# Zero matmuls ahead of and between the first transposes, alpha loaded one step ahead, small loads later

## The chip, the cores and the metric

One core of a Trainium2 chip runs the kernel. TensorE (PE, with its weight loads shown as PEld), VectorE (DVE), ScalarE (ACT), GpSimd (POOL) and SyncE (SP) run side by side and wait for each other by semaphores; SP issues nearly all loads and stores to the DMA queue. The metric is device microseconds of one execution, lower is better.

## The reference

A linear attention with a decaying state feeds a mixture of experts with one expert per token. Batch 4, 8 heads, 768 tokens, 48 channels per head; 3072 tokens of 384 channels and 8 experts of 384 x 1024 x 384 behind it. All inputs are float32.

```python
for t in range(S):
    state = alpha[:, :, t, :, None] * state + np.einsum('bhd,bhe->bhde', k[:, :, t], v[:, :, t])
    y[:, :, t] = np.einsum('bhd,bhde->bhe', q[:, :, t], state)
...
logits = x @ w_gate + modality_bias[modality_id]
e_idx = np.argmax(logits, axis=1)
...
for e in range(E):
    mask = e_idx == e
    h = np.maximum(x[mask] @ w1[e], 0.0)
    out[mask] = gate_w[mask, None] * (h @ w2[e])
```

## The kernel before

The attention is done in 24 chunks of 128 tokens (six to each batch), in a software pipeline of 24 steps. Each chunk needs four loads of 192 KB: alpha, k, q and v, as 128 tokens by 8 heads by 48 channels. Step s of the loop (line 836) does this:

- issue the loads of a later chunk (line 838), ahead of all else of the step;
- `decay_in(s)`: TensorE transposes the four tiles of alpha chunk s (`trans`, L238) and the result is copied to `X` by ScalarE (L245; for chunk 0 by VectorE). In step 1 it comes behind `scale(0)`;
- `scale(s-1)`: TensorE transposes k and q of chunk s-1, VectorE multiplies them with the running products of alpha (L277 gives `kh`, L280 gives `qh`);
- `rows(s-3)`, and `logits_rows` in every second step: transposes of earlier results;
- `natural(s-1)`: TensorE transposes `kh` back (L286);
- `decay(s)`, `decay_back(s)`, `guard(s)`: two scans on VectorE (L250, L261) and a check of alpha on ScalarE (L265);
- `logits(s-3)` in every second step, from step 4 on (L368, reads `wgp`), `state(s-2)` (L318; nothing for the first chunk of a batch), `scores(s-1)` (L298), `outputs(s-2)` (L325, needs v of chunk s-2), `update(s-1)` (L343, needs v of chunk s-1).

TensorE, VectorE and ScalarE run in the order in which this is written out (`manual_schedule`). SP and GpSimd run in an order that a planner makes from the written order and its own idea of when things are ready. Each engine's instructions run strictly in its order, so one that waits holds back everything behind it.

Ahead of the loop, SP issues the load of `wgs` (the gate weights in a layout that only a fallback path reads, `logits_pe`), then twelve chunk loads in the order a0 k0 q0 a1 v0 k1 q1 a2 v1 k2 q2 v2, then six small ones: `wgp` in four pieces (the gate weights that `logits` reads), `mi` (modality of each token) and `mbb` (the bias table); the last two are read by `bias_table` in step 6. In step s > 0 it loads all four tensors of chunk s+2 (PF is 3). There are four buffers each for alpha, k and q and six for v, so chunk 3 has a buffer of its own from the start.

The router's work on earlier chunks is spread over the later steps. After the loop the experts run: weights are fetched as soon as the router knows which, and the matmuls of L987 to L1008 fill TensorE for the rest of the time.

`y` names a PSUM buffer of two banks that exists once; `state` takes it in step 2 for the first time.

## Time and profile before

| | |
|---|---|
| runs | 379.71, 376.4 and 588.9 us, median 379.71 |
| profiled execution | 379.2 us, of it 377.2 us span |
| mean granted TensorE clock | 0.988 |
| TensorE busy | 359.6 us, 95% of the span |
| VectorE, ScalarE, GpSimd busy | 59%, 50%, 40% |
| DMA | 59.19 MB, mean 157 GB/s |

Times in rows of the trace count from the start of the span. A row of the time line gives start, length, engine, line, operation, output tile from input tiles, and how many instructions were merged into it; in brackets stands the idle time of the engine ahead of it and what ended that. `SPq` rows are issues of the DMA queue: their length is that of the issue, not of the transfer. A matmul's row contains the time until its result is out, so neighbouring matmuls overlap; the distance of their starts is what one costs. PEclk is the clock granted to TensorE as a share of full speed.

### The profile page before, as it was taken

The page shows a single profiled execution, that of the slowest core. Times are in us where ns is not written, and L with a number is a line of the kernel's source. Part 1 is how long each engine was busy: PE and PEld are TensorE (multiplying, and loading weights), DVE is VectorE, ACT ScalarE, POOL GpSimd, SP SyncE. Part 2 cuts the span into 40 slices and gives each one's busy share as a digit, 9 for nine tenths or more (in the row PEclk, how much of TensorE's full clock was granted, in tenths as well). Part 3 has the DMA queues.
Part 4 walks back from the last instruction along what each step waited for, and adds up shares of the span by engine and source line. Part 5 has one row for each costly group of instructions (what it writes and reads, how often), then busy time and mean ns, then how long its engine had stood idle before and what let it go on. Part 6 is the DMA issues. An engine that isn't in the chain of part 4 may idle for free. (4 is left out here: it accounts for less than half of the span.)

```text
span 377.2 us, 9342 instructions
## 1 busy us (share of the span) xinstructions
PE 359.6 (95%) x3652; PEld 319.9 (85%) x3652; DVE 223.9 (59%) x454; ACT 189.4 (50%) x367; POOL 149.7 (40%) x218
## 2 busy tenths in 40 slices
PE   4979999999999989999999999999999999999993
PEld 3778789888888978789998899899889989888993
DVE  5765988977988988895846604641552366026400
ACT  2447677767767746344745415432552445145310
POOL 9434335434454544346155424612631273220022
PEclk9989999999999989999999999999999999999998
DMA  9999999999989792948847434621733373200011
GB/s 128 131 170 163 191 193 196 182 182 198 191 179 185 153 370 73 365 137 318 305 113 235 126 119 150 223 89 63 257 99 105 115 219 117 85 28 27 1 44 49
DMA packets 123246, 59.19 MB, mean 157 GB/s; under 512 B 103377, under 2 KB 114696, under 8 KB 123192
## 3 DMA queue, kind: packets, MB, share of 16 engines
q1 hardware_dynamic: 119224, 48.84, 57.1%
q0 software_dynamic: 3968, 9.65, 7.6%
q8 instruction: 31, 0.51, 0.6%
q14 instruction: 23, 0.19, 0.2%
HBM read 49.03 MB, written 9.50 MB: 155 GB/s over the span
## 5 line engine op out<-in xcount | busy, mean ns | idle before, releaser
L303 POOL TENSOR_SCALAR_AFFINE_SELECT scT<-scT 128x512 f32<-128x512 f32 x48 | 38.3, 821 | 72.4 <-ACT scT L302 72.4
L953 POOL DMA_INDIRECT out_dram<-os,odx x23 | 23.1, 1003 | 109.8 <-ACT os L1021 93.6
L987 PE MATMUL sc<-w2H,hH 128*128 128x384 f32 x192 | 65.0, 338 | 0.0
L989 PE MATMUL sc<-w2H,hL 128*128 128x384 f32 x192 | 64.2, 334 | 0.0
L988 PE MATMUL sc<-w2L,hH 128*128 128x384 f32 x192 | 64.1, 334 | 0.0
L823 DVE TENSOR_TENSOR w1L<-w1r,w1H 128x768 fp32r<-128x768 f32 x24 | 22.0, 956 | 67.2 <-ACT w1H L821 67.2
L1006 PE MATMUL tr<-xH,w1H 128*128 128x512 f32 (+1 forms) x144 | 53.8, 374 | 0.0
L1008 PE MATMUL tr<-xH,w1L 128*128 128x512 f32 (+1 forms) x144 | 53.5, 372 | 0.0
L1007 PE MATMUL tr<-xL,w1H 128*128 128x512 f32 (+1 forms) x144 | 53.5, 371 | 0.0
L815 DVE SCALAR_TENSOR_TENSOR hL<-tr,hH 128x512 fp32r<-128x512 f32 x47 | 32.4, 688 | 31.4 <-ACT hH L813 31.3
L813 ACT ACTIVATE hH<-tr 128x512 fp32r<-128x512 f32 x47 | 28.1, 598 | 45.4 <-PE tr L1008 42.0
L1021 ACT ACTIVATE os<-sc,gg 128x384 f32<-128x384 f32 x23 | 13.4, 583 | 67.0 <-PE sc L989 40.3
L987 PEld LDWEIGHTS sc<-w2H,hH 128*128 128x128 f32 x192 | 36.1, 188 | 1.1 <-issue 1.0
L988 PEld LDWEIGHTS sc<-w2L,hH 128*128 128x128 f32 x192 | 36.1, 188 | 0.0
L989 PEld LDWEIGHTS sc<-w2H,hL 128*128 128x128 f32 x192 | 36.0, 188 | 0.0
L686 POOL DMA_INDIRECT gg<-gd,idx x25 | 27.0, 1081 | 21.2 <-DMA gd<-gs 14.2
L302 ACT COPY scT<-sc 128x512 f32<-128x512 f32 x48 | 25.8, 590 | 13.6 <-PE sc L298 13.6
L261 DVE TENSOR_TENSOR_SCAN Fw<-X,DF 128x516 f32<-128x516 f32 x24 | 31.1, 1295 | 0.8
L680 POOL DMA_INDIRECT xg<-xd,idx x25 | 26.8, 1072 | 11.6 <-issue 5.2
L1008 PEld LDWEIGHTS tr<-xH,w1L 128*128 128x128 f32 x144 | 27.1, 188 | 4.7
L1007 PEld LDWEIGHTS tr<-xL,w1H 128*128 128x128 f32 x144 | 27.1, 188 | 4.6
L1006 PEld LDWEIGHTS tr<-xH,w1H 128*128 128x128 f32 x144 | 27.1, 188 | 4.7
(242 smaller groups left out, 682.9 us busy)
## 6 DMA issues: line engine op xcount, KB each, us to landing
w1r<-in_moe_w_dram SPq DMA_DIRECT2D x16, 768.0 KB, 4.6
w2r<-in_moe_w_dram SPq DMA_DIRECT2D x16, 768.0 KB, 7.8
nat_a<-in_alpha_dram SPq DMA_DIRECT2D x24, 192.0 KB, 4.1
nat_k<-in_k_dram SPq DMA_DIRECT2D x24, 192.0 KB, 5.5
nat_q<-in_q_dram SPq DMA_DIRECT2D x24, 192.0 KB, 4.2
vt<-in_v_dram SPq DMA_DIRECT2D x24, 192.0 KB, 5.1
xd<-xs SPq DMA_DIRECT2D x24, 192.0 KB, 3.9
xg<-xd,idx POOLq DMA_INDIRECT x25, 4.6
```

The source lines that it names most:

```text
L261: vec.tensor_tensor_scan(Fw, x[:, :-1], d, 0.0, op0=ALU.mult, op1=ALU.add)
L303: pool.affine_select(s, s, [[0, NP], [1, P]], ALU.is_ge, 0.0, base=0, channel_multiplier=-1)
L680: pool.indirect_dma_start(xg[x][:, u], None, xd[0:rows], IOA(idx[:, c : c + 1], 0), bounds_check=rows - 1, oob_is_err=False)
L686: pool.indirect_dma_start(gg[x][:, u : u + 1], None, gd[0:rows], IOA(idx[:, c : c + 1], 0), bounds_check=rows - 1, oob_is_err=False)
L813: act.activation(hH, hp, AF.Relu)
L815: vec.scalar_tensor_tensor(hL, hp, 0.0, hH.bitcast(F32), op0=ALU.max, op1=ALU.subtract)
L987: pe.matmul(op, hH[:, us] if f is None else hH[:, f, us], wH, start=first, stop=False)
L988: pe.matmul(op, hH[:, us] if f is None else hH[:, f, us], wL, start=False, stop=False)
L989: pe.matmul(op, hL[:, us] if f is None else hL[:, f, us], wH, start=False, stop=final)
L1006: pe.matmul(hp, wH[:, d, fs], XH[:, d, :n], start=(d == 0), stop=False)
L1007: pe.matmul(hp, wH[:, d, fs], XL[:, d, :n], start=False, stop=False)
L1008: pe.matmul(hp, wL[:, d, fs], XH[:, d, :n], start=False, stop=(d == ND - 1))
```

## The change

The load of `wgs` moves into the fallback path, which does not run with these inputs. Thirteen chunk loads are issued ahead of the loop, alpha one chunk further than the rest: a0 k0 q0 a1 v0 a2 k1 q1 v1 a3 k2 q2 v2. In the loop alpha of chunk s+3 and k, q, v of chunk s+2 are loaded. The `wgp` loads move into step 1, behind that step's chunk loads, and those of `mi` and `mbb` into step 2.

In addition VectorE clears a bf16 tile `still` of 128 x 512 ahead of its other work, and TensorE multiplies it with its own first 128 columns: seven times ahead of everything else, and once behind each of the first seven transposed chunks (a0, k0, q0, a1, a2, k1, q1). The products go to a tile `idle` in the `y` buffer, which nothing reads.

```diff
     wgs = cp.tile([P, ND, E], F32, name="wgs")
-    sp.dma_start(wgs, wg.rearrange("(c p) e -> p c e", p=P))
-
+    for n in "a0 k0 q0 a1 v0 a2 k1 q1 v1 a3 k2 q2 v2".split():
+        load(int(n[1]), n[0])
+    still = ac.tile([P, 4 * P], BF16, name="still")
+    vec.memset(still, 0.0)
+    idle = ps.tile([P, 4 * P], F32, name="y")
+
+    def warm(n):
+        for _ in range(n):
+            pe.matmul(idle, still[:, :P], still, start=True, stop=True)
+
+    warm(7)
     wgp = ac.tile([P, 2, 2, 32], F32, name="wgp")
     pool.memset(wgp, 0.0)
-    for n in "a0 k0 q0 a1 v0 k1 q1 a2 v1 k2 q2 v2".split():
-        load(int(n[1]), n[0])
-    for c in range(2):
-        ...
     mi = ac.tile([NU, P, 2], I32, name="mi")
-    sp.dma_start(mi.rearrange("t p w -> t (p w)"), ...)
     mbb = ac.tile([P, NM, E], F32, name="mbb")
-    sp.dma_start(mbb, mb.unsqueeze(0).broadcast_to([P, NM, E]))
+    def load_gate():
+        ...
+    def load_modality():
+        ...
@@ trans
+        if i < 2 or (i == 2 and n == "a"):
+            warm(1)
         return p
@@ general (fallback path)
+        sp.dma_start(wgs, wg.rearrange("(c p) e -> p c e", p=P))
@@ the loop over steps
     for s in range(NU):
+        if s > 0 and s + PF < NU:
+            load(s + PF, "a")
         if s > 0 and s + PF - 1 < NU:
-            load(s + PF - 1)
+            load(s + PF - 1, "kqv")
+        if s == 1:
+            load_gate()
+        if s == 2:
+            load_modality()
```

`load_gate` and `load_modality` hold the loads taken out above, four and two.

## The prediction

> **What bounds the kernel now.** First the page's list of engines. TensorE is busy for nearly the whole span, so time is gained by taking idle time, or slow time, away from TensorE. (The page's chain that ended last is only 1 us long here and says nothing.)

> ```profile
> PE 359.6 (95%) x3652; PEld 319.9 (85%) x3652; DVE 223.9 (59%) x454; ACT 189.4 (50%) x367; POOL 149.7 (40%) x218
> ```

> Second, TensorE's own time line. A row is a run of matmuls: start, length, line, how many, and in brackets the idle time before it. I measure from one start to the next, since the ends overlap.

> ```profile
> 4.96 1.08 PE L238 MATMUL tr<-ident,nat_a 128*128 128x128 f32 x4 [4.96 <-POOL zr L184]
> ...
> 10.38 1.12 PE L286 MATMUL tr<-ident,kh 128*128 128x128 f32 x4 [0.70 <-DVE kh L277]
> 11.42 1.99 PE L298 MATMUL sc<-qh,kh 48*64 48x128 f32 x32
> 13.34 1.09 PE L343 MATMUL kv<-vt,knat 128*64 128x48 f32 x16
> 14.36 1.12 PE L238 MATMUL tr<-ident,nat_a 128*128 128x128 f32 x4
> ...
> 17.21 0.63 PE L286 MATMUL tr<-ident,kh 128*128 128x128 f32 x4 [0.24 <-DVE kh L277]
> ...
> 19.72 0.62 PE L343 MATMUL kv<-vt,knat 128*64 128x48 f32 x16
> 22.41 0.63 PE L238 MATMUL tr<-ident,nat_a 128*128 128x128 f32 x4 [2.06 <-DMA nat_a<-in_alpha_dram]
> ...
> 29.27 0.65 PE L238 MATMUL tr<-ident,nat_a 128*128 128x128 f32 x4
> ...
> 30.63 0.62 PE L356 MATMUL tr<-ident,yt 128*128 128x128 f32 x4
> 31.14 0.66 PE L286 MATMUL tr<-ident,kh 128*128 128x128 f32 x4
> 31.73 0.64 PE L368 MATMUL kv<-yt,wgp 128*32 128x256 f32 x8
> 32.30 0.67 PE L318 MATMUL y<-qh,T 64*64 64x128 f32 x16
> 32.78 1.06 PE L298 MATMUL sc<-qh,kh 48*64 48x128 f32 x32
> 33.77 1.09 PE L325 MATMUL y<-scT,vt 128*64 128x128 f32 x16
> 34.70 0.62 PE L343 MATMUL kv<-vt,knat 128*64 128x48 f32 x16
> 35.25 0.66 PE L238 MATMUL tr<-ident,nat_a 128*128 128x128 f32 x4
> ```

> Step 4 runs from 29.27 to 35.25 with no gap: 5.98 us of TensorE work set its length. The beginning is different: transposing four tiles takes 1.12 us at 10.38 and 0.63 us at 17.21, and there is an idle stretch of 2.06 us ahead of alpha chunk 3, the first work of step 3 (22.41). So the first 17 us run on a slow clock, and at 22.41 a load is late.

> Third, the windows. Columns: window, its length, busy time of PE, PEld, DVE, ACT, POOL (instructions), granted clock, DMA share, GB/s. The cuts are 3.41 us apart, where the recorded clock changes.

> ```profile
> 6.37:9.78 3.41, 3.03 (x12) 1.86 (x10) 3.27 (x6) 0.60 (x3) 3.25 (x11) 1.00 1.50 166
> 9.78:13.19 3.41, 2.81 (x36) 2.31 (x36) 3.31 (x6) 1.71 (x4) 2.65 (x9) 1.00 1.50 163
> 13.19:16.60 3.41, 3.41 (x32) 3.17 (x28) 0.85 (x2) 1.93 (x4) 1.71 (x3) 1.00 1.46 160
> 20.02:23.43 3.41, 1.35 (x22) 1.25 (x19) 0.50 (x1) 1.09 (x4) 2.59 (x4) 1.00 0.95 151
> 23.43:26.85 3.42, 3.42 (x33) 3.09 (x35) 3.17 (x6) 1.58 (x4) 0.00 (x0) 0.50 1.19 178
> 40.50:43.91 3.41, 2.56 (x33) 2.19 (x33) 3.31 (x9) 2.43 (x7) 2.22 (x4) 1.00 1.22 204
> 132.66:136.07 3.41, 1.78 (x36) 1.11 (x37) 3.24 (x12) 1.05 (x3) 0.36 (x1) 1.00 1.03 380
> 136.07:139.49 3.42, 3.42 (x56) 3.09 (x58) 3.32 (x14) 1.53 (x6) 1.89 (x2) 0.50 1.06 384
> ```

> Read each row with the next one. After windows with TensorE busy for 1.35 of 3.41 us (40%) and 1.78 (52%) the clock is 0.50 for one window; after 2.56 (75%) it stays at 1.00. From 0.50 it comes back after a window that is full (3.42). The 1.00 of the first three rows can't be right: by the durations above TensorE was at about half speed until some 16.6. Windows filled to 89% (3.03) and 82% (2.81) did not open the clock; the full one, 13.19 to 16.60, did.

> Fourth, the load queue, for the late load.

> ```profile
> 0.81 0.44 SPq L136 DMA_DIRECT2D wgs<-in_moe_w_gate_dram  x1
> 1.30 0.48 SPq L133 DMA_DIRECT2D nat_a<-in_alpha_dram  x1
> ...
> 10.39 1.14 SPq L133 DMA_DIRECT2D nat_k<-in_k_dram  x1
> ...
> 12.76 1.14 SPq L133 DMA_DIRECT2D vt<-in_v_dram  x1
> 14.02 2.49 SPq L144 DMA_DIRECT2D wgp<-in_moe_w_gate_dram  x4
> 16.55 0.43 SPq L149 DMA_DIRECT2D mi<-in_moe_modality_id_dram  x1
> 17.42 0.43 SPq L133 DMA_DIRECT2D nat_a<-in_alpha_dram  x1
> ```

> Alpha chunk 3 is issued at 17.42, behind twelve chunk loads (1.19 us apart) and six small loads that hold the queue from 14.02 to 17.42; TensorE gets it at 22.41, 4.99 us after its issue.

> **The change, part by part.** *Loads.* The wgs load leaves the front: the first chunk is issued up to 1.30 - 0.81 = 0.49 us earlier (at least 0, if it then waits for something else). Alpha 3 becomes the tenth load; the tenth was issued at 10.39, so it goes at about 9.9 and lands near 14.9.

> *Warm matmuls at the front.* VectorE first clears `still`; its first memset now is this:

> ```profile
> 0.99 0.49 DVE L155 MEMSET DR<- 128x517 f32 x1 [0.99 <-PEq L1220]
> ```

> With as long a one the seven matmuls start near 1.5, and all transposes stand behind them. No bf16 matmul of 512 columns is in this trace. Nearest are fp32r ones of 384 columns:

> ```profile
> 175.68 0.33 PE L989 MATMUL sc<-w2H,hL 128*128 128x384 f32 x1
> ...
> 177.76 0.34 PE L989 MATMUL sc<-w2H,hL 128*128 128x384 f32 x1
> ```

> Twelve starts in 2.08 us are 0.173 us each, hence 0.23 us for 512 columns at full clock and 0.46 at half (a bound below is 0.17, as if columns cost nothing; above, 0.46 at any clock). Seven at half clock are 3.2 us: 1.5 to 4.7. The first alpha lands up to 0.49 before 4.96, so its transposes start near 4.7: I take 0.25 us of gain at the front (bounds 0 and 0.49). From 1.5 on TensorE is without a gap of note until the clock opens, after the first full window of 3.41 us: between 4.9 and 8.3, since the start of the windows need not lie the same in another execution.

> *Steps 0 to 2.* In step 0 and the first half of step 1 VectorE is what is late (the brackets at 10.38 and 17.21 name its `kh`). Its scan ahead of the second kh:

> ```profile
> 12.58 1.23 DVE L261 TENSOR_TENSOR_SCAN Fw<-X,DF 128x516 f32<-128x516 f32 x1
> ```

> So a faster TensorE gains nothing before `kh`, and the four warm matmuls among the first transposes lie beside this wait. The transposes of kh start at 10.38 - 0.25 = 10.13. From there at full clock, with step 4's lengths: natural 0.59 (31.14 to 31.73; was 1.04), scores 0.99 (was 1.92), update 0.55 (was 1.02), so step 2 begins at 12.26 instead of 14.36. Its three transposed chunks take 1.36 (29.27 to 30.63) plus three warm matmuls of 0.23, to 14.3. That is just behind the second kh, which VectorE can make by then (its scan ends at 12.58 + 1.23 - 0.25 = 13.56). From natural to the end of update took 17.21 to 20.27 (19.72 + 0.55), 3.06 us, and with 0.1 for qh step 3 begins at 17.5. Here chunk 3 (landed at 14.9) is no longer late. So the gain to this point is 22.41 - 17.5 = 4.9 us, of which 2.1 are the late load and 2.8 the clock and the front.

> *Step 3.* It took 29.27 - 22.41 = 6.86 us, half of it at half clock. With no idle stretch ahead the clock need not fall: its length is then step 4's without the logits, 5.98 - 0.57 = 5.41. Gain 1.45.

> *The moved small loads.* The wgp loads come after 17 chunk loads instead of 12: issued from 14.02 + 5 x 1.19 - 0.49 = 19.5 to 22.0. The last row gives what they took from issue to landing (from the view of the tile wgp); the first, of the queue's time line, is a chunk load that held the queue 1.0 us longer than the usual 1.1:

> ```profile
> 19.59 2.15 SPq L133 DMA_DIRECT2D vt<-in_v_dram  x1
> ```

> ```profile
> DMA to landing us min/median/max: 3.0/3.5/3.9
> ```

> So the last, issued near 21.6 (22.0 less the 0.43 of one issue), lands at 24.6 to 25.5. Logits of step 4 want it at 17.5 + 5.41 + 2.46 (29.27 to 31.73) = 25.4. All of step 4 from state on stands behind them in TensorE's order. The bounds of the wait are 0 and 1.1 (the late landing with one such long issue ahead of it); I take the middle, 0.5. The other step 4 and 5 loads have 2 us or more in hand by the same count, and mi and mbb, wanted in step 6, more.

> `idle` lies in the `y` buffer of PSUM, which only TensorE writes before step 2, in its own order: no cost. After step 4 TensorE is the engine that sets the pace (95% busy), so it all stays: 4.9 + 1.45 - 0.5 = 5.85 us. The profiled execution took 379.2 us (span 377.2 and 2.0 around it); that gives **373.4 us**. The median of the runs shown, 379.71, is 0.5 higher, the lowest, 376.4, 2.8 lower; with changes under 2% (7.6 us) a measurement of this kernel can't well be told from no change.

> **Rivals.** *The clock opens and falls shut again.* With a full clock TensorE waits for loads 1.2 us apart and for kh: three tiles of 0.44 to 0.49 with their warm matmuls of 0.23 make 2.1 of 3.41 us, some 61%. Between 52% (fell) and 75% (held) the trace doesn't say. One full window at half clock costs half of its 3.41 us, 1.7: 375.1. I give this rival 22%. [...]

> *The work doesn't count.* If zeros or transposes are no activity for the clock, windows with a third of such work stay shut, and the clock opens only at about 20. Then step 2 has its old times, 14.36 to 17.21, a front gain of 0.25 and three half-speed warm matmuls (1.38): natural starts at 18.3, takes 1.04 and scores some 1.6, outputs and update 1.5 (33.77 to 35.25), and step 3 begins at 22.4 as before. Only its 1.45 is gained: 377.8. For transposes the row 23.43 to 26.85 speaks against it (most of its first 2.5 us are transposes, and it opened the clock). For zeros no row speaks. Chance 12%. [...]

> *The small loads get late* (the other side). SP's order is a planner's. If it puts wgp behind the next four chunk loads too, it lands 4.8 us later, at 30.2; TensorE stands 4.8 us in step 4, that window closes the clock (1.7), and 6.5 us are lost against 6.35 gained: 379.4. One chunk load more, 1.2, and it is 380.6, slower than before. It decides from five loads on. For it: nothing else protects the order. Against: in this trace SP kept the program's order until step 4. Chance 6%.

> *More is gained.*

> ```profile
> 134.81 0.65 PE L286 MATMUL tr<-ident,kh 128*128 128x128 f32 x4 [1.63 <-DVE kh L277]
> ```

> This wait of 1.63 us, whole in the window from 132.66, closes the clock. Moved by 5.85 us against the windows it may be split between two and hold the clock: 1.7 us more, 371.7. A gap of 1.63 fits in 3.41 whole in 52% of positions, but a split one need not spare it. Chance 15%.

> **How the numbers follow.** The forecast itself, 372.5 to 374.5, gets 45%. Range: from 370.8 (more is gained, with 0.49 at the front and no wait for wgp) to 377.8 (the work doesn't count); outside remain the late loads and some of the spread between executions. Faster by over 2% means below 372.1: the "more" rival and a few runs of the main case, 0.2. Slower by over 2% needs 387: 0.02. Within 2%: 0.78.

> **What would show it.** Right: four transposes in about 0.63 us from the second half of step 1 on; clock records of 1.00 from 5 to 8 us on with no 0.50 ahead of 100 us; alpha chunk 3 transposed near 17.5 with no wait on its DMA; step 4 begun near 22.9. Wrong: scores at 1.9 us in step 1 (clock not open), a wait of L368 on wgp in step 4, or warm matmuls that delay the first transposes past 5 us.

## The result

After the change the kernel takes 374.81 us, the median of 20 runs (372.68 to 378.09); the kernel before, run beside it, 377.81 (20 runs). The ratio is 0.992, with a 95% interval of 0.989 to 0.995: 3.0 us or 0.8% faster, which is inside the 2% called no change. The prediction was 373.4 us in a range of 370.8 to 377.8, with a chance of 0.78 for "within 2%"; the time lies just above the 372.5 to 374.5 of the forecast itself. The profiled execution after took 375.57 us (span 373.6, mean clock 0.989), 3.6 us less than that before (379.2, 377.2, 0.988); the sum had promised 5.85.

**The profile after.** The page's list of engines has hardly moved: TensorE is 0.5 us less busy, although it now makes 14 zero matmuls more.

```profile
PE 359.1 (96%) x3666; PEld 317.0 (85%) x3666; DVE 224.8 (60%) x455; ACT 189.0 (51%) x367; POOL 151.6 (41%) x218
```

TensorE's time line after, read as that of before. L249 are the transposes (L238 before), L144 the zero matmuls, L299 the transposes of `kh`, L381 the logits.

```profile
1.26 3.17 PE L144 MATMUL y<-still 128*128 128x512 bf16 x7 [1.26 <-DVE still L139]
4.22 1.06 PE L249 MATMUL tr<-ident,nat_a 128*128 128x128 f32 x4
...
7.78 0.63 PE L249 MATMUL tr<-ident,nat_a 128*128 128x128 f32 x4
...
10.03 0.63 PE L299 MATMUL tr<-ident,kh 128*128 128x128 f32 x4 [1.40 <-DVE kh L290]
...
12.22 0.66 PE L249 MATMUL tr<-ident,nat_a 128*128 128x128 f32 x4
...
17.48 0.66 PE L249 MATMUL tr<-ident,nat_a 128*128 128x128 f32 x4
...
22.89 0.66 PE L249 MATMUL tr<-ident,nat_a 128*128 128x128 f32 x4
...
25.35 0.64 PE L381 MATMUL kv<-yt,wgp 128*32 128x256 f32 x8
...
28.87 0.66 PE L249 MATMUL tr<-ident,nat_a 128*128 128x128 f32 x4
...
36.24 0.66 PE L249 MATMUL tr<-ident,nat_a 128*128 128x128 f32 x4 [1.78 <-DMA nat_a<-in_alpha_dram]
...
38.81 0.64 PE L381 MATMUL kv<-yt,wgp 128*32 128x256 f32 x8 [0.41 <-DVE mt L228]
```

Steps 3, 4 and 5 begin at 17.48, 22.89 and 28.87. Before it was 22.41, 29.27 and 35.25, so 4.93 us are gained at step 3 and 6.38 from step 4 on. Then comes a wait that the prediction doesn't have: at 36.24 alpha chunk 6 is 1.78 us late, and the gain falls to 4.53 (step 6 began at 40.77 before).

The load queue after shows why.

```profile
9.58 1.31 SPq L133 DMA_DIRECT2D nat_a<-in_alpha_dram  x1
...
20.11 3.58 SPq L155 DMA_DIRECT2D wgp<-in_moe_w_gate_dram  x4
23.79 0.38 SPq L133 DMA_DIRECT2D nat_a<-in_alpha_dram  x1
...
26.41 1.37 SPq L161 DMA_DIRECT2D mi<-in_moe_modality_id_dram  x1
...
28.23 0.43 SPq L133 DMA_DIRECT2D vt<-in_v_dram  x1
28.75 0.39 SPq L860 DMA_DIRECT2D xd<-zr  x1
29.18 0.25 SPq L861 DMA_DIRECT2D gd<-zr  x1
29.53 0.39 SPq L133 DMA_DIRECT2D nat_k<-in_k_dram  x1
30.02 1.15 SPq L133 DMA_DIRECT2D nat_q<-in_q_dram  x1
31.27 1.07 SPq L133 DMA_DIRECT2D nat_a<-in_alpha_dram  x1
```

The alphas shown are chunks 3, 5 and 6. The program writes alpha 6 ahead of k, q and v of chunk 5; the planner put it behind them and behind the two stores of `zr`. So alpha 6 goes at 31.27, only 0.53 us sooner than before (31.80), while TensorE comes for it 6.3 us sooner, and gets it 4.97 us after its issue.

Two windows after, columns as before, at the place where the clock had fallen in the kernel before (136.07):

```profile
126.70:130.10 3.40, 1.77 (x31) 1.62 (x30) 3.23 (x9) 0.81 (x2) 0.83 (x2) 1.00 0.63 157
130.13:133.54 3.41, 3.41 (x48) 2.27 (x50) 3.27 (x18) 1.45 (x4) 2.24 (x2) 0.50 1.03 387
```

A window filled to 52% is again followed by one at half clock: in this execution the dip only moved with the work. From step 6 on TensorE runs 4.5 to 5.0 us ahead of the kernel before until a gather of rows is 0.49 us late at 208.59; its last matmul is 4.30 us ahead, and 0.7 us go between that and the end of the span, around the last scatter.

### The profile page after: what moved, and what is told of

Same layout as the page of the kernel before. It is cut to its first block, busy times and chain, and to the rows that moved or that the text cites. A ratio compares the mean times of both kernels' runs of the same rounds, so it can differ in the third digit from the quotient of the medians.

```text
span 373.6 us, 9370 instructions
## 1 busy us (share of the span) xinstructions
PE 359.1 (96%) x3666; PEld 317.0 (85%) x3666; DVE 224.8 (60%) x455; ACT 189.0 (51%) x367; POOL 151.6 (41%) x218
## 5 line engine op out<-in xcount | busy, mean ns | idle before, releaser
L829 DVE SCALAR_TENSOR_TENSOR hL<-tr,hH 128x512 fp32r<-128x512 f32 x47 | 32.4, 689 | 31.5 <-ACT hH L827 31.3
L699 POOL DMA_INDIRECT gg<-gd,idx x25 | 26.6, 1063 | 21.9 <-DMA gd<-gs 14.9
```

Source lines behind the costliest of these rows:

```text
L699: pool.indirect_dma_start(gg[x][:, u : u + 1], None, gd[0:rows], IOA(idx[:, c : c + 1], 0), bounds_check=rows - 1, oob_is_err=False)
L829: vec.scalar_tensor_tensor(hL, hp, 0.0, hH.bitcast(F32), op0=ALU.max, op1=ALU.subtract)
```

## The experiments

What had to be told apart: how much of the gain belongs to the zero matmuls and how much to the loads; and what made alpha 6 late, the planner's order (theory O), the small loads that now stand in the middle of SP's queue (S), or the bandwidth of the transfers (B). The letters are those of the expectations below. Ratios hold against the kernel before on the same chip: 380.53 us for the first four kernels, 379.33 for the next four, 380.56 for the last four.

**The loads without zero matmuls.** Edit against the kernel after:

```diff
-    warm(7)
...
-        if i < 2 or (i == 2 and n == "a"):
-            warm(1)
```

> Without any zero matmul (still, idle and all of them left out; alpha ahead and small loads later stay). Theory A, the clock and the load add up, but the wait for alpha 6 at step 6 takes part back: the clock opens only at 13 to 17 us, step 3 begins at about 20.0 instead of 17.5, step 4 at 25.4, step 5 at 31.4, step 6 at 37.0 with no wait for alpha 6, which is issued near 31 and lands near 36.2. Against the changed kernel only 0.7 us are lost (about 375.5 where that has 374.8). Theory B, the zero matmuls are worth what they gain by step 5: 2.5 us or more lost, 377.5. Theory C, they do nothing, since the loads alone set the start: step 3 at 17.5, no difference.

Measured: 377.16 us, ratio 0.9939 [0.9906, 0.9973]. Time line of TensorE (L240 are the transposes):

```profile
20.18 0.66 PE L240 MATMUL tr<-ident,nat_a 128*128 128x128 f32 x4
...
37.09 0.65 PE L240 MATMUL tr<-ident,nat_a 128*128 128x128 f32 x4
```

Without zero matmuls the clock opens (its record in the trace begins) at 17.52 instead of 7.25, and step 3 begins 2.70 us later than in the kernel after, but step 6 only 0.85 later, since it doesn't wait for alpha 6: theory A of the expectation, which had 20.0 and 37.0. Of what the zero matmuls bring up to step 3, 1.78 us are handed back as a wait. Whether the rest shortens the whole isn't shown: the interval of this ratio overlaps that of the kernel after (0.989 to 0.995), which was measured at another time.

**Only the seven at the front; only those between.**

```diff
 front only:                                   between only:
-        if i < 2 or (i == 2 and n == "a"):    -    warm(7)
-            warm(1)
```

> Only the seven zero matmuls at the front, none between the transposes. Theory A: the clock needs a window that is full to some 95% or more. Between the first transposes the gaps are 0.1 to 0.3 us of 1.2, so by A it does not open at 7 to 8 us but at 13 to 17, and step 3 begins at about 20, as without any. Rival: seven at the front are enough, the clock opens by 8.3 and holds, and step 3 begins at 16.8 to 17.3, earlier than with the matmuls between. Time by A about 375.5, by the rival 374.8 (the wait for alpha 6 levels it).

> Only the seven zero matmuls between the transposes, none at the front. Theory A: from 4.2 us on TensorE is full at half clock (transposes 0.9 plus 0.42 per 1.2 us of load), so the clock opens after the first full window, at 7.6 to 11.0, and step 3 begins at 17.5 to 18.5: the front ones are worth 0 to 1 us at step 3 and nothing behind the wait for alpha 6. Rival: without the front the windows never fill, the clock opens at 13 to 17, and the half-speed zero matmuls cost on top: step 3 at 21 to 22.

Measured: front only 376.77 us, 0.9899 [0.9863, 0.9934]; between only 376.21, 0.9901 [0.9868, 0.9934]. The totals don't tell them apart; the traces do. Windows of the front-only kernel:

```profile
2.64:6.05 3.41, 3.41 (x13) 1.78 (x11) 0.95 (x6) 1.94 (x3) 3.41 (x26) 1.00 1.32 188
6.05:9.46 3.41, 1.53 (x10) 0.84 (x8) 3.31 (x5) 0.64 (x2) 3.25 (x11) 1.00 1.49 166
9.46:12.87 3.41, 2.86 (x36) 2.30 (x36) 3.31 (x6) 1.19 (x3) 3.25 (x7) 0.50 1.50 163
```

The full first window opens the clock at 6.05; the next is filled to 45%, and from 9.46 it is shut, until 16.29. Step 3 begins at 19.91, little better than with none (20.18). That is theory A's figure but not its mechanism: by A the clock would not have opened at all before 13. Its limit of 95% was the author's estimate, and no run shows it: 3.17 of 3.41 us (93%) opened the clock in the row from 1.18 below, and 3.41 of 3.41 did not in the row from 10.69 of the last section. Time line of the between-only kernel:

```profile
17.12 0.66 PE L248 MATMUL tr<-ident,nat_a 128*128 128x128 f32 x4
...
35.77 0.65 PE L248 MATMUL tr<-ident,nat_a 128*128 128x128 f32 x4 [1.19 <-DMA nat_a<-in_alpha_dram]
```

Here the clock opens at 7.86 and holds, and step 3 begins at 17.12, no later than with the seven in front as well (17.48). So the seven in front open the clock but don't keep it; those between do both. And alpha 6 is late at step 6 here too, by 1.19 us (1.78 in the kernel after).

**Zero matmuls on the kernel before.** The `still`, `warm(7)` and `warm(1)` lines of the diff, and none of the rest.

> The kernel before with the zero matmuls alone (loads as before). Theory A: TensorE is ready for step 3 at about 17.7 but alpha 3 still comes at 22.4; over 4 us of idle time close the clock again, and step 4 begins at 29.3 as before. Time as before (ratio 0.998 to 1.002). Rival: what the clock gains up to step 3, 2.5 us, comes through (ratio 0.993).

Measured: 381.27 us, 1.0029 [0.9993, 1.0065]: no gain. TensorE's time line:

```profile
21.43 0.94 PE L247 MATMUL tr<-ident,nat_a 128*128 128x128 f32 x4 [2.82 <-DMA nat_a<-in_alpha_dram]
...
28.38 0.66 PE L247 MATMUL tr<-ident,nat_a 128*128 128x128 f32 x4
```

With the old order of loads the wait for alpha 3 grows by 0.76 us (2.82, was 2.06). Two windows of this kernel: the first holds nothing but zero matmuls, and the clock opens behind it, at 4.59; the second holds the wait, TensorE fills 18% of it, and the clock is 0.50 from 21.66 to 25.07.

```profile
1.18:4.59 3.41, 3.17 (x7) 0.89 (x7) 1.55 (x9) 0.00 (x0) 3.36 (x24) 1.00 0.71 119
18.24:21.66 3.42, 0.60 (x16) 0.47 (x13) 0.56 (x1) 0.77 (x3) 2.64 (x4) 1.00 0.76 133
```

Step 4 begins 0.89 us earlier than before (29.27), which theory A didn't have, and the median shows none of it. In these runs the zero matmuls gain nothing without the loads (1.0029); the loads gain without them (0.9939).

**SP in the written order; the small loads on ScalarE's queue; both.** The kernel after ran beside them, unchanged, for comparison.

```diff
-    manual = {mybir.EngineType.PE, mybir.EngineType.DVE, mybir.EngineType.Activation}
+    manual = {mybir.EngineType.PE, mybir.EngineType.DVE, mybir.EngineType.Activation, mybir.EngineType.SP}
```

```diff
 load_gate, load_modality, now called ahead of the loop:
-                sp.dma_start(
+                act.dma_start(
```

> The changed kernel once more, as the measure for the runs beside it on the same chip. Ratio to the kernel before 0.989 to 0.995; step 3 at 17.5, step 6 at about 36 behind a wait of 1 to 2 us for alpha 6.

> SP too runs in the written order (one word more in manual_schedule), so alpha 6 is issued ahead of k, q and v of chunk 5 instead of behind them. Theory O, the planner's order made alpha 6 late: it is issued at about 28.2, lands by 33, the 1.8 us wait at step 6 is gone, step 6 begins at 34.5 and the kernel is 1.8 us faster than the changed one. Theory B, the DMA queue as a whole is behind at that point: then k or q of chunk 5, now issued last, are waited for instead, for 1 us or more, and the time stays.

> The six small loads are issued by ScalarE at the start instead of by SP in steps 1 and 2; SP's order stays the planner's. Theory S, the small loads hold SP's queue (20.1 to 23.8 and 26.4 to 28.2, 5.3 us, with the DMA engines nearly idle for 3 of them) and so make alpha 6 late: it is issued at about 26 to 28 instead of 31.3, no wait at step 6, 1.8 us faster than the changed kernel. Theory B, the chunk loads alone fill the DMA queue (26 chunk loads at 1.19 us ahead of alpha 6 are 31.7): issued at 31 or later, the wait at step 6 stays at 1 to 2 us, no gain. In either case the first chunk loads may land 0.3 to 0.6 us later, since the small loads share the engines with them.

> Both edits together: SP in the written order and the small loads by ScalarE at the start. Theories O and S: as the better of the two alone, 1.8 us faster than the changed kernel, no wait of TensorE on a load in steps 3 to 8. Theory B: a wait on k or q of chunk 5 or 6 of 1 us or more stays.

Measured: unchanged 373.82 us, 0.987 [0.983, 0.991], a little better than expected; SP as written 372.68, 0.983 [0.9788, 0.9872]; small loads by ScalarE 373.15, 0.9845 [0.9799, 0.989]; both 372.7, 0.9841 [0.9799, 0.9883]. The issue of alpha 6 and the start of step 6, in the time lines of the unchanged kernel, of the one with the small loads on ScalarE's queue, and of the one with SP as written:

```profile
31.83 0.97 SPq L133 DMA_DIRECT2D nat_a<-in_alpha_dram  x1
36.45 0.66 PE L249 MATMUL tr<-ident,nat_a 128*128 128x128 f32 x4 [2.00 <-DMA nat_a<-in_alpha_dram]
```

```profile
28.95 1.39 SPq L133 DMA_DIRECT2D nat_a<-in_alpha_dram  x1
34.39 0.66 PE L252 MATMUL tr<-ident,nat_a 128*128 128x128 f32 x4
```

```profile
28.32 0.37 SPq L133 DMA_DIRECT2D nat_a<-in_alpha_dram  x1
36.00 0.66 PE L249 MATMUL tr<-ident,nat_a 128*128 128x128 f32 x4
```

In the second and the third the wait is gone. The third is not as clean as the second, since its clock fell early (below) and TensorE came for alpha 6 only at 36.00; but issued at 28.32, with the 4.97 us of the kernel after, it would be there at 33.3 (an estimate), ahead of 34.4. So to remove either cause, O or S, is enough, each holds a part, and B falls: the same bytes arrive in time. B had also miscounted: 24 and not 26 chunk loads stand ahead of alpha 6, which at 1.19 us each from 0.81 on makes 29.4, near the 28.95 measured. With the small loads gone from the queue step 6 begins at 34.39, 2.70 us ahead of the kernel without zero matmuls (37.09), as at step 3 (17.47 and 20.18): up to there all they bring is kept.

The expectations had 1.8 us. Of the 2.06 us between 36.45 and 34.39, 1.63 are left at step 7 (42.08 and 40.45), since the logits of step 6 wait 0.85 instead of 0.41 us for `mt`. At the front, with the small loads on ScalarE's queue, k0, q0 and a1 are transposed at 5.73, 6.95 and 8.32, in the unchanged kernel at 5.43, 6.40 and 7.68: 0.3 to 0.6 us later, as the expectation had it, and `kh` comes at 10.02 in both. The medians gain 0.7 to 1.1 us over the unchanged kernel, and the intervals overlap, so that this saves time in total is not shown by them alone. The runs differ with their clock: with SP as written one took 371.11 us at a mean clock of 0.996 and one 375.65 at 0.986. Among the runs at 0.994 and above the unchanged kernel has 373.54 and 373.60, the three others 371.02 to 372.91 (eight runs): below it, but few. In the profiled execution of SP as written the clock fell early, to 0.50 from 11.94 to 15.35, behind this window:

```profile
8.53:11.94 3.41, 2.03 (x47) 1.60 (x48) 3.34 (x6) 1.77 (x5) 3.25 (x8) 1.00 1.49 164
```

**Alpha not ahead; the small loads ahead of the loop again.**

```diff
 no ahead:                                     small loads first:
-        if s > 0 and s + PF < NU:             +    load_gate()
-            load(s + PF, "a")                 +    load_modality()
...                                            -        if s == 1: ...
-            load(s + PF - 1, "kqv")           -        if s == 2: ...
+            load(s + PF - 1)
```

The first has the twelve loads in front in their old order, too.

> The changed kernel without alpha one chunk ahead (twelve chunk loads first, then all four of chunk s+2 in step s); zero matmuls and small loads later stay. Alpha 3 is then the thirteenth load, issued at 13.3, landed at 18.2 to 18.5, and TensorE is ready at 17.5: step 3 begins 0.7 to 1.0 us later. Theory L, the wait for alpha 6 levels what comes before it: alpha 6 has the same place in SP's order (30th), step 6 begins at about 36.2 as in the changed kernel, time equal within 0.5 us. Rival: being ahead is worth its 0.8 us or more to the end.

> The changed kernel with the six small loads back ahead of the loop, behind the thirteen chunk loads; zero matmuls and alpha ahead stay. Alpha 3 is still early, step 3 at 17.5. Alpha 4 and k of chunk 3 go at about 18 and land near 23, wanted at 22.9 and 23.4: waits of 0 to 1 us in step 4. Theory L: step 6 again begins near 36, time equal to the changed kernel within 0.5 us. Rival: the small loads' place is worth 1 us or more.

Measured: 377.94 us, 0.9938 [0.9905, 0.997], and 377.5, 0.9931 [0.9899, 0.9963]. Their time lines:

```profile
13.15 0.63 PE L249 MATMUL tr<-ident,nat_a 128*128 128x128 f32 x4 [0.87 <-DMA nat_a<-in_alpha_dram]
19.00 0.66 PE L249 MATMUL tr<-ident,nat_a 128*128 128x128 f32 x4 [0.55 <-DMA nat_a<-in_alpha_dram]
26.00 0.63 PE L249 MATMUL tr<-ident,nat_a 128*128 128x128 f32 x4 [1.52 <-DMA nat_a<-in_alpha_dram]
...
37.48 0.66 PE L249 MATMUL tr<-ident,nat_a 128*128 128x128 f32 x4
```

```profile
24.66 0.67 PE L252 MATMUL tr<-ident,nat_a 128*128 128x128 f32 x4 [2.00 <-DMA nat_a<-in_alpha_dram]
...
37.76 0.66 PE L252 MATMUL tr<-ident,nat_a 128*128 128x128 f32 x4
```

Without alpha ahead it is late three times, 2.94 us in all; with the small loads first alpha 4 is 2.00 us late and the clock falls behind it (half clock from 25.1 to 28.5). Both reach step 6 some 1.2 to 1.5 us behind the kernel after. So in the traces each edit of the loads is worth something at step 6 although another wait remains; the idea that the loads level out to the same step 6 whatever their order (L in the expectations) missed that. In the totals it isn't shown: the kernel after did not run beside these two, and the intervals overlap.

**The last gap filled; all of it together.** Ahead of the first `kh` TensorE still stands idle for 1.40 us.

```diff
-            warm(1)
+            warm(6 if i == 1 and n == "a" else 1)
```

> The changed kernel with five more zero matmuls behind the transposes of alpha 1, in the 1.4 to 1.8 us in which TensorE waits for the first kh (5 x 0.22 us). The runs so far show the clock fall behind a window with 2.03 us of work and hold behind one with 2.01, so this gap decides by chance. With the fill no record of 0.50 ahead of 100 us; step 3 at 17.5, step 6 still at 36 behind the wait for alpha 6. Time 0 to 0.5 us below the changed kernel. Rival: the fill delays the transposes of kh and costs 0.3 us.

> All edits that took a wait away: SP in the written order, small loads by ScalarE at the start, and the five zero matmuls in the gap. No 0.50 ahead of 100 us, no wait of over 0.6 us of TensorE on a load up to step 8, step 6 at 34.5 to 35. Expected 1.5 to 2.5 us below the changed kernel, ratio to the kernel before 0.981 to 0.986 on a chip where the changed kernel has 0.987 to 0.992.

The second adds to this SP in the written order and the small loads on ScalarE's queue. Measured: 377.2 us, 0.9919 [0.9888, 0.995], and 375.45, 0.9891 [0.9851, 0.9932]. Time line of the first:

```profile
10.02 0.63 PE L299 MATMUL tr<-ident,kh 128*128 128x128 f32 x4 [0.29 <-DVE kh L290]
```

The gap shrinks from 1.40 to 0.29 us without delaying the transposes of `kh`, and alone this gains nothing that could be measured. The combined kernel has the lowest median of its chip, reaches step 6 at 34.36 and shows no half clock until 369.99 us, but its ratio misses the 0.981 to 0.986 that were expected. Against the profile of the kernel after it is 2.5 us ahead at 135 us and 0.1 at 172: it gives 2.4 us back in between, 0.9 of them in one wait ahead of a `kv` matmul at 148.81. All eight kernels of the first and the last group have one such wait of 0.9 us, the four of the middle group and the two of the main comparison have none. So it goes with the group, perhaps with the chip, and not with an edit; its cause stays open.

## Why the prediction held, and where it was wrong

**Front and clock: right.** The seven matmuls take 3.17 us, 0.42 apart at half clock (0.46 predicted; 0.22 at full, 0.23 predicted). The first transposes come at 4.22 instead of the predicted 4.7, so the front gains 0.74 and not 0.25: without the seven, between-only, alpha 0 is there at 4.00, which is 0.96 sooner than 4.96. The term was too small because it counted only the 0.49 us of earlier issue, but this has no effect, since `kh` sets the next time (10.03, predicted 10.13). The clock opens at 7.25 (4.9 to 8.3 predicted). Step 2 begins at 12.22 (12.26), step 3 at 17.48 (17.5), with no wait for alpha 3.

**Step 3 and the gate weights.** Step 3 takes 5.41 us as predicted, gain 1.45. For `wgp` 0.5 us were taken from bounds of 0 and 1.1. It was 0: the logits run at 25.35 with no wait, the lower bound. (Between-only reached it 0.35 sooner and did wait, 0.21.) By step 4 the gain was thus 6.38 where the sum without that wait had 6.35.

**The step that failed: "After step 4 ... it all stays".** It rested on "the other step 4 and 5 loads have 2 us or more in hand", and no line counted step 6's. The trace of before had what was needed. Its load queue, the start of step 6 in its TensorE time line, and the last line of the view of the tile `nat_a`, which gives the times from issue to landing of the alpha loads for which the trace has them (alpha 6 is not among them):

```profile
31.80 0.45 SPq L133 DMA_DIRECT2D nat_a<-in_alpha_dram  x1
```

```profile
40.77 0.66 PE L238 MATMUL tr<-ident,nat_a 128*128 128x128 f32 x4
```

```profile
DMA to landing us min/median/max: 3.2/4.1/5.1
```

With 6.35 us gained step 6 would begin at 34.4. Alpha 6, issued at 31.80, would land between 35.0 and 36.9 by this view (an estimate): 0.6 to 2.5 us late. Only a place further ahead in the queue would have saved it, and that was SP's planner's to give; the prediction says that the planner may move `wgp`, but took "one chunk ahead" for granted in every step. The wait measured 1.78 us. The "2 us or more" was not there for step 5 either: alpha 5 is issued at 23.79 in the kernel after and used at 28.87, 5.08 us later, hardly more than the 4.97 that alpha 6 took.

**The last 0.9 us.** From 4.53 at step 6 the gain grows by 0.44, as TensorE waits 0.41 instead of 0.85 us for `mt`; the gather at 208.59 takes 0.7 (0.49 of it as the wait in the row) and the end 0.7. None of these was in the sum, and the two losses were not tested.

**The size against the median.** In profiles 3.63 us are gained, in medians 3.0. The profiled execution of before contains two windows at half clock, and its 379.2 us lies above the median of the 20 runs, 377.81. The step of 1.45 us is a dip that part of the executions of the kernel before may not have; the runs list only a mean clock for each, so how often it falls at 23.4 isn't shown. So the predicted time came within 1.4 us although the gain was 2.85 us too large against that of the medians: the base, 379.2, was 1.4 us too high, and half of the error cancelled. That half is luck.

**The rivals.** "The work doesn't count" falls, for each kind of work by itself: on the kernel before the clock opens at 4.59 behind a window of zero matmuls alone (the row 1.18:4.59 above), and without zero matmuls at 17.52 behind a window of transposes alone (the row 14.10:17.52 below). "The clock opens and falls shut again" didn't happen in the profiled execution but did in that of SP as written, whose beginning is almost the same: there the window from 8.53, filled with 2.03 of 3.41 us, was followed by half clock, while the one from 7.25 of the kernel after, with 2.01, was not. "The small loads get late" named the right queue and the wrong load: they were in time, and made alpha 6 late. "More is gained" missed in the profiled execution: the dip moved along (126.70 to 133.54). Five kernels show none there. In four of them (no zero matmuls, small loads first, ScalarE's queue with SP as written, all together) the wait of some 1.6 us for `kh` lies across two windows, each filled with 2.44 to 2.75 us, as this rival had it. In the fifth, alpha not ahead, it lies whole in one window, and the clock holds all the same:

```profile
129.90:133.31 3.41, 1.78 (x36) 1.21 (x40) 3.31 (x11) 1.14 (x4) 0.88 (x1) 1.00 0.97 285
```

## What to carry to other kernels

When a change pulls an engine forward by x us, go on along its loads until one is found that has less than x in hand, and count each from its issue in the trace; what exceeds that is lost at the first that is late, however far behind the edit (here 1.78 us of 6.38, at alpha 6). A program order is worth only what the scheduler of that queue keeps of it (alpha 6 went at 31.27 in the planner's order, at 28.32 in the written one): read the issued order, and put small loads on a queue that nothing urgent shares (2.88 us earlier for alpha 6, below). Zero matmuls at the front alone opened the clock at 6.05 and it was shut again at 9.46; those between opened it at 7.86, and it was still open at 24.92. So look at the gaps between the first matmuls, and not only at what comes ahead of them.

## What the runs showed of the hardware

```profile
7.25:10.66 3.41, 2.01 (x17) 1.18 (x19) 3.31 (x7) 0.58 (x1) 3.17 (x11) 1.00 1.50 166
34.56:37.97 3.41, 1.73 (x16) 1.69 (x16) 2.01 (x5) 0.91 (x3) 1.77 (x4) 1.00 0.89 166
```

```profile
10.69:14.10 3.41, 3.41 (x51) 2.71 (x50) 2.49 (x4) 2.29 (x6) 3.33 (x8) 1.00 1.50 163
14.10:17.52 3.42, 3.40 (x16) 2.94 (x15) 1.45 (x3) 0.82 (x2) 1.31 (x3) 1.00 1.50 163
```

It held behind 1.73 of 3.41 us (51%, the wait for alpha 6), 1.78 (52%, above) and 2.01 (59%), and fell behind 1.53, 1.77 and, with SP as written, 2.03 (59%). So these busy times, which are themselves modelled, show no single limit. What fills the windows differs. The one with 1.73 is 16 transposes of 128 x 128; the one with 2.03 holds the 32 small matmuls of the scores (48 x 64); the one with 1.77 has 16 matmuls of 2 columns; and the full one that opened nothing holds scores and an update, at half clock, for 2.9 us. No experiment varied what such small work counts for. The longest gap in a window behind which the clock fell in the first 150 us was 2.82 us (the wait for alpha 3 with zero matmuls on the kernel before). The moment of opening differed between two executions of the same kernel: 7.25 in one, 5.35 in the other.

Here the small loads cost time in the queue rather than in the transfer. The four `wgp` loads held SP from 20.11 to 23.69, and from 22 to 25 the DMA engines stood nearly still (share 0.16, against 1.35 from 16 to 20). Two windows of the kernel after, columns as above (the last two are DMA share and GB/s), one with chunk loads issued one behind the other and one behind the `wgp` loads:

```profile
16.00:20.00 4.00, 4.00 (x60) 3.61 (x57) 3.16 (x7) 3.01 (x8) 3.47 (x5) 1.00 1.35 158
22.00:25.00 3.00, 3.00 (x44) 2.78 (x41) 1.79 (x3) 2.05 (x6) 2.66 (x4) 1.00 0.16 17
```

17 GB/s against 158: at the second rate these bytes take 0.3 us, so by this estimate some 2.7 of the 3 us could have gone to chunks. Moved to ScalarE's queue the small loads let alpha 6 be issued 2.88 us earlier (28.95 against 31.83).
